# The first transform of batches 1 to 7, from twelve split passes over 128 rows to three sessions of folded 64x64 tiles

## The chip, the cores and the metric

One core of one Trainium2 chip runs the whole kernel in one launch. The metric is the device time of a launch in microseconds (us); lower is better. TensorE (PE) multiplies, VectorE (DVE), ScalarE (ACT) and GpSimd (POOL) work elementwise, and SyncE (SP) issues nearly all transfers, in program order.

## The reference, cut to what matters

```python
X = np.fft.rfft(x, axis=1)                      # x: 8 batches x 3072 x 256, float32
y = np.fft.irfft(X * (filt_r + 1j * filt_i), n=3072, axis=1)
x = y.reshape(8 * 3072, 256)
h = np.maximum(x @ w_in, 0.0)                   # w_in 256 x 2048
x = h * h @ w_out                               # w_out 2048 x 256
# then a soft mixture of 8 experts with 32 slots over all 24576 rows:
#   softmax over the rows gathers slot inputs, softmax over the slots hands the results out
```

The transform of 3072 points is done in two stages, 128 x 24. The first stage is the one that changes: for each of the 24 columns n, a real transform of 128 points over the rows, as a product with a constant 128 x 128 matrix of cosines and sines.

## The kernel before, in words

The main loop (`for P in range(NP + 2)`) runs over 384 pairs. A pair makes two blocks of 128 hidden columns for a chunk of 512 rows: `layer` issues three matmuls per call and four calls per pair, into the two PSUM banks p0 and p1, one bank each per block. `square` (ACT, and POOL for the second block), `turn_h` (a DVE transpose), `logit` (PE, `mm L`) and once per chunk of eight pairs the softmax work (`gather`, `slot_in`, `accum`) follow.

Everything else is put between those matmuls by hand. Time in the schedule is counted in half steps: a pair is two of them, six `layer` matmuls each, and a chunk is 16. A batch is six chunks, 96 half steps. `fft_events` writes, for batch b, when each piece is issued (`put(T, function, ...)`), relative to the start of batch b-1, whose matmuls run meanwhile. Four lists (`dsp`, `late`, `fft`, `w`) are walked by `run_streams` in order of due time. A piece that needs PSUM banks (the table `take`) is issued only when so many of the five side banks are free; otherwise it and all later ones that need banks wait.

Each engine executes its instructions in that written order, SP its transfers too: a store that waits for its data holds up the loads written behind it.

The first stage before, per batch: `load_x` brings x in six transfers of 512 KB (128 partitions, 4 columns n). Twelve times, every 0.9 to 1.5 half steps: `split_x` makes a high part h on ACT and a remainder lo on POOL (both float32r, a reduced format that TensorE runs faster than float32); `mm_a` issues three matmuls of 128x128 by 512 columns into one bank (lines 159 to 161: matrix high times h, matrix low times h, matrix high times lo); `evac_a` copies the bank to SBUF on ACT; `store_a` writes 256 KB to a DRAM scratch S. Later `load_s2` reads S back transposed for the second stage: `mm_b`, `filt` (DVE), `join` (POOL), `mm_g2`, `evac_g2`, `store_g2`, each four times a batch (j = 0 to 3). Batch 0 goes another way, in the head, and has no part in this.

The tiles f8 (1 MB, three buffers) hold x, the filter, S and the output of the second stage in turn; the tiles u (256 KB, eight buffers) held h, lo, the evacuated bank and the products of `filt`.

Of the kernel before, what the change touches and what calls it, by code (L numbers as in the profile page):

```python
# [6 lines left out]
F32 = mybir.dt.float32  # L7
F32R = mybir.dt.float32r
U32 = mybir.dt.uint32
ACTF = mybir.ActivationFunctionType  # L10
ALU = mybir.AluOpType
# [4 lines left out]
D = 256  # L16
N1 = 128
N2 = 24
# [20 lines left out]
def body(tc, x, cA, cAf, fwp, fwd, ivp, inv, flt, cst, w_in, w_out, phi, w1, w2, out):  # L39
    nc = tc.nc  # L40
    sync = nc.sync
    act, vec, gps, pe = nc.scalar, nc.vector, nc.gpsimd, nc.tensor

    def pool(name, bufs=1, space=None, side=None):
        kw = {} if space is None else {"space": space}
        p = tc.tile_pool(name=name, bufs=bufs, side=side, **kw)
        return p, p.__enter__()
# [4 lines left out]
    const_c, const = pool("const")  # L52
# [4 lines left out]
    first_c, first = pool("first")  # L57
# [5 lines left out]
    def F(i):  # L63
        return ST["F0"] + ST["dF"] * i
# [18 lines left out]
    def put0(t, fn, *a):  # L83
        ev0[round(t, 3)].append((fn, a))


    cst_t = const.tile([128, C_END], F32, name="cst_t")
    ca_t = const.tile([128, 2, 128], F32R, name="ca_t")
    ss_t = const.tile([128, 128], F32R, name="ss_t")
    phi_t = const.tile([128, 2, NS], F32, name="phi_t")  # L90
    cI = cst_t[:, C_I:C_I + 128]
# [17 lines left out]
    def side():  # L109
        if G["nsd"]:  # L110
            return G["ps"].tile([128, 512], F32, tag="sd", name="sd", bufs=G["nsd"])
        k = free.pop(0)
        p = G["ps"].tile([128, 512], F32, tag=f"s{k}", name="sd")
        taken[id(p)] = k, p
        return p

    def done(p):

        if id(p) in taken:
            free.append(taken.pop(id(p))[0])  # L120


    def fft_events(b, pl, put, A0, dA, TB, TG, n, st):
        xv = x[b].rearrange("(p n) d -> p n d", n=N2)

        def bank0(k):
            return G["ps"].tile([128, 512], F32, tag=f"q{k}", name="sd", bufs=1)

        def one(tag, shape):
            return pl().tile(shape, F32, tag=tag, name=tag.rstrip("0123456789"), bufs=1)  # L130

        def small(k=None):
            if b == 0:
                return one(k, [128, 2, D])
            return pl().tile([128, 2, D], F32, tag="u", name="u", bufs=n["u"])

        def load_x(sl):
            t = st["x2"] if sl % 2 else wide()
            st["x2"], t = t, t[:, sl % 2]
            st["x", sl] = t  # L140
            sync.dma_start(out=t, in_=xv[:, 4 * sl:4 * sl + 4, :])

        def load_u(u):
            sl, n = divmod(2 * u, 4)
            st["x", sl] = st["big"][:, sl]
            sync.dma_start(out=st["x", sl][:, n:n + 2], in_=xv[:, 2 * u:2 * u + 2, :])

        def split_x(u):
            src = st["x", u // 2][:, 2 * (u % 2):2 * (u % 2) + 2, :]
            h = small().bitcast(F32R)  # L150
            lo = small().bitcast(F32R)
            act.activation(out=h, in_=src, func=ACTF.Copy)  # L152
            gps.tensor_tensor(out=lo, in0=src, in1=h.bitcast(F32), op=ALU.subtract)  # L153
            st["xs", u] = (h, lo)

        def mm_a(u):
            p = side()
            h, lo = st.pop(("xs", u))
            pe.matmul(p, ca_t[:, 0, :], h, start=True, stop=False)  # L159
            pe.matmul(p, ca_t[:, 1, :], h, start=False, stop=False)  # L160
            pe.matmul(p, ca_t[:, 0, :], lo, start=False, stop=True)  # L161
            st["a", u] = p

        def evac_a(u):
            if u == 0:
                st["S"] = dram.tile([N1, N2, D], F32, tag="S", name="S")
            p = st.pop(("a", u))
            o = small()
            act.activation(out=o, in_=p.rearrange("p (a d) -> p a d", d=D), func=ACTF.Copy)
            done(p)  # L170
            st["o", u] = o

        def store_a(u):
            sync.dma_start(out=st["S"][:, 2 * u:2 * u + 2, :], in_=st.pop(("o", u)))


        def wide():
            return pl().tile([128, 2, 4, D], F32, tag="f8", name="f8", bufs=n["f"])
# [201 lines left out]
        if b == 0:  # L380
# [21 lines left out]
            for i in range(8):  # L402
                put((.38, .4, .42, .44)[i] if i < 4 else F(i - 4) + 2.6, load_f, i)
                T = (16.8, 17.2, 20, 22.4, 24.9, 25.3, 27.4, 27.8)[i]
                for s in range(2):
                    put(T + .1 * s, mm_t, i, s)
                    put(T + .3 + .1 * s, evac_t, i, s)
                put(F(i) - 1.2, mm_b, i)
# [4 lines left out]
                put((29.85, 32.3, 34.75, 37.2, 39.9, 41.5, 44.6, 40.5)[i], mm_g, i)  # L413
                T = (31.1, 33.6, 36.1, 38.6, 41.2, 44.7, 45.9, 42.4)[i]
                for c in range(4):
                    put(T, evac_g, i, c)
                put(T + 1.25, store_g, i)
            return

        for sl in range(6):  # L420
            put(A0 + 2 * sl * dA - 5, load_x, sl)
        for u in range(12):
            T = A0 + u * dA
            put(T - 2, split_x, u)
            put(T, mm_a, u)
            put(T + 0.5, evac_a, u)
            put(T + 2.5, store_a, u)
        for j in range(4):
            T = TB[j]
            for k in range(2):  # L430
# [9 lines left out]
            T = TG[j]  # L440
# [423 lines left out]
    streams = {"dsp": [], "late": [], "fft": [], "w": []}  # L864
    heads = dict.fromkeys(streams, 0)

    take = {"warm": 1, "mm_a": 1, "mm_b": 2, "mm_g": 4, "mm_g2": 4, "mm_ai": 1, "gather": 1, "slot_in": 4, "turn_wo": 1, "mm_wf": 1}

    def takes(fn, a):
        if fn is conv_wo and a[1] in (6, 7, 10, 11):  # L870
# [3 lines left out]
    def stream(nm, o=0):  # L874
        def put(t, fn, *a):
            streams[nm].append((t + o, fn, a))
        return put
# [33 lines left out]
        G["fft_c"], G["fft"] = pool("fft", 2)  # L911

    def load_const():
        gps.dma_start(out=ca_t, in_=cA)
        gps.dma_start(out=ss_t, in_=cst[:, C_SS:C_SS + 128])
        sync.dma_start(out=phi_t, in_=phi.rearrange("(k p) s -> p k s", p=128))

# [26 lines left out]
    with tc.manual_schedule():  # L944
        put, late = stream("fft"), stream("late")
        st = {}
        put0(43.3, load_const)
        fft_events(0, lambda: first, put0, 0, 0, 0, 0, None, st)
        out_events(0, st, late)
        def wput(t, *a):  # L950

# [7 lines left out]
        for j in range(4):  # L959
            ts, ops, h, lo = WI[j]  # L960
# [20 lines left out]
        for b in range(1, NB):  # L981
            st = {}
            if b == 1:
                when = (27, .9, [49, 54.5, 65.5, 76.5], [53, 61.5, 70.5, 81.5])
            elif b == 2:
                when = (-14, 1, [5.5, 21.5, 37.5, 53.5], [17.5, 33.5, 49.5, 65.5])
            else:
                when = (-25, 1.5, [1.5, 21.5, 37.5, 53.5], [17.5, 33.5, 49.5, 65.5])
            fft_events(b, lambda: G["fft"], stream("fft", 96 * (b - 1)), *when, dict(f=3, u=8, c=2), st)
            out_events(b, st, late)  # L990
        for c in range(NCH - 1):
# [48 lines left out]
        for P in range(NP + 2):  # L1040
# [15 lines left out]
            if P > NP - 8:  # L1056
                j, odd = divmod(P - NP + 7, 2)
# [17 lines left out]
        st, evac_l, gather, emax, expo, rescale, turn_e, turn_l, slot_in, row_max, row_exp, row_out, store_c = dispatch_events(NCH - 1, None)  # L1075
# [15 lines left out]
        for r in range(4):  # L1091
# [4 lines left out]
            out=fz, in0=run["z"], scalar=st["sc"], in1=st["zb"], op0=ALU.mult, op1=ALU.add  # L1096
# [18 lines left out]
        parts = hs[0] + [dsp.tile([128, 512], F32, tag=t, name="sp") for t in ("lp", "et")]  # L1115
        for r in range(4):
            p = st["S"][r]
# [18 lines left out]
        p = bank("s0")  # L1136
        for j in range(16):
# [3 lines left out]
                start=(j < 4), stop=(j >= 12), tile_position=(0, 32 * c4),  # L1141
# [3 lines left out]
        p = bank("s1")  # L1145
# [31 lines left out]
        def layer2(r, h):  # L1177
# [25 lines left out]
        p = bank("s4")  # L1203
# [6 lines left out]
            out=sr[64:128], in0=p[64:128, 0:D], in1=sr[64:128].bitcast(F32), op=ALU.subtract  # L1210
# [5 lines left out]
        for g in range(NG):  # L1216
            b, o = divmod(g, N2 // 4)
# [3 lines left out]
            for h in range(2):  # L1221
                p = bank(("s0", "s1", "s2", "s3")[ops % 4]).rearrange("p (a d) -> p a d", d=D)
# [19 lines left out]
def _constants():  # L1242
    import numpy as np

    def split(a):
        a32 = a.astype(np.float32)
        h = (a32.view(np.uint32) & np.uint32(0xFFFFF000)).view(np.float32)
        return h, (a - h.astype(np.float64)).astype(np.float32)

    p = np.arange(N1)  # L1250
    j, ri = p // 2, p % 2
    n1 = np.arange(N1)
    ph = 2 * np.pi * ((n1[:, None] * j[None, :]) % N1) / N1
    alt = (-1.0) ** n1
    a = np.where(ri[None, :] == 0, np.cos(ph), -np.sin(ph))
    a[:, 0] = 1.0
    a[:, 1] = alt
    cA = np.stack(split(a), axis=1)
    cAf = a.reshape(N1, 8, 2, 4, 2).transpose(0, 1, 3, 2, 4).reshape(N1, N1)
    ci = np.where(ri[None, :] == 0, np.cos(ph), -np.sin(ph)).T.copy()  # L1260
    ci[0] = 1.0
# [3 lines left out]
    ks = np.zeros((64, 24), np.int64)  # L1265
    ang = np.zeros((64, 24), np.int64)
    for jj in range(64):
        for q in range(24):
            if jj == 0:
                ks[jj, q] = 128 * q if q < 12 else 64 + 128 * (q - 12)  # L1270
                ang[jj, q] = ks[jj, q]
            elif q < 12:
                ks[jj, q] = ang[jj, q] = jj + 128 * q
            else:
                ks[jj, q] = 128 - jj + 128 * (q - 12)
                ang[jj, q] = N - ks[jj, q]
    fw = np.zeros((32, 96, 128))
    iv = np.zeros((32, 128, 96))
# [1 line left out]
    for t in range(32):  # L1280
        for jj in range(2):
            jb = 2 * t + jj
            rr = 48 * jj
            for q in range(24):
# [4 lines left out]
                if jb == 0:  # L1289
                    src = r0 if q < 12 else r1  # L1290
# [25 lines left out]
    for jb in range(64):  # L1316
        t, jj = divmod(jb, 2)
# [77 lines left out]
```

## Time and profile before

| | us |
|---|---|
| median of 3 runs | 1933.9 (1932.58 to 1937.23) |
| the profiled execution, whole | 1935.35 |
| its span, first to last instruction | 1933.6 |
| PE busy in the span | 1900.2 (98%) |
| DVE / ACT / POOL busy | 1196.9 / 1066.5 / 708.9 |
| mean granted TensorE clock | 0.997 of full |

The profile lists busy time by engine, a chain of waits followed back from the last instruction, and groups of instructions by source line. Its matmul ends are modelled, so the distance from one matmul's start to the next one's start says more than a matmul's duration.

### The profile page before, as it was taken

Reading aid. Unit: us, or ns where it says so; the run is one execution under the profiler, and the core shown is the slowest. Engines: PE = TensorE matmul, PEld = TensorE weight load, DVE = VectorE, ACT = ScalarE, POOL = GpSimd, SP = SyncE. Lnnn points to the kernel's source line nnn. Section 1 sums busy time; section 2 is a strip of 40 time slices with the busy share of each in tenths; the row PEclk is TensorE's granted clock in tenths of the full one; section 3 lists DMA queues with packets and bytes.
Section 4 is the critical chain, followed back from the end, with each engine's and each line's share of the span. In section 5 each row is a group of like instructions: output and inputs, shape, how many; then the busy total and the mean of one; then the engine's idle time right before and its main releaser. Section 6 shows DMA issues by size and latency. Waiting matters only on the chain.

```text
span 1933.6 us, 44644 instructions
## 1 busy us (share of the span) xinstructions
PE 1900.2 (98%) x18448; PEld 1321.0 (68%) x18448; DVE 1196.9 (62%) x2209; ACT 1066.5 (55%) x1974; POOL 708.9 (37%) x765
## 2 busy tenths in 40 slices
PE   8999999999999999999999999999999999999987
PEld 6776667666776776766766676676766667676655
DVE  7855656575566646656566655665565655565658
ACT  6764555555654565555555465455745545455535
POOL 4052453343434343334433344333533422222224
PEclk9999999999999999999999999999999999999999
DMA  8634544342334134233424234322442414000589
GB/s 305 208 132 114 164 149 125 81 119 95 117 99 110 48 133 130 77 87 109 131 63 129 69 117 137 88 77 62 151 99 79 110 30 145 13 26 14 163 320 382
DMA packets 139787, 232.27 MB, mean 120 GB/s; under 512 B 13888, under 2 KB 91840, under 8 KB 139584
## 3 DMA queue, kind: packets, MB, share of 16 engines
q1 hardware_dynamic: 138568, 228.08, 38.5%
q8 instruction: 145, 2.38, 0.5%
q10 hardware_dynamic: 728, 1.15, 0.2%
q14 instruction: 58, 0.48, 0.1%
q0 software_dynamic: 288, 0.20, 0.1%
HBM read 151.77 MB, written 77.59 MB: 119 GB/s over the span
## 4 chain that ended last, share of the span: by engine, by line
PE 93%; DVE 3%; DMA 2%; issue 1%; ACT 1%; SPq 0%; ACTq 0%; DVEq 0%
PE p L531 19%; PE p L533 18%; PE p L532 18%; PE sd L683 11%; PE L L558 9%; PE sd L470 4%; PE sd L292 3%; PE sd L211 3%; PE sd L159 1%; PE sd L160 1%; PE sd L161 1%; DVE ct L1029 1%; PE pt L1018 1%; PE pt L1225 1%; DMA x<-x 1%
## 5 line engine op out<-in xcount | busy, mean ns | idle before, releaser
L538 ACT ACTIVATE h<-p 128x512 f32<-128x512 f32 x768 | 459.6, 599 | 547.8 <-PE p L533 524.7
L542 POOL TENSOR_TENSOR h<-h 128x512 f32<-128x512 f32 x375 | 390.7, 1042 | 940.8 <-ACT h L538 855.9
L549 DVE STREAM_TRANSPOSE hT<-h 128x512 f32<-128x512 f32 x768 | 513.9, 692 | 316.7 <-ACT h L540 315.5
L531 PE MATMUL p<-xo,wiH 128*128 128x512 f32 x1534 | 627.6, 409 | 0.6 <-ACT h L538 0.6
L533 PE MATMUL p<-xo,wiL 128*128 128x512 f32 x1534 | 605.9, 395 | 0.0
L532 PE MATMUL p<-xo,wiH 128*128 128x512 f32 x1534 | 605.8, 395 | 0.0
L531 PEld LDWEIGHTS p<-xo,wiH 128*128 128x128 f32 x1534 | 289.1, 188 | 136.4 <-issue 69.6
L533 PEld LDWEIGHTS p<-xo,wiL 128*128 128x128 f32 x1534 | 289.1, 188 | 68.6
L532 PEld LDWEIGHTS p<-xo,wiH 128*128 128x128 f32 x1534 | 289.7, 189 | 57.3
L540 ACT ACTIVATE h<-h 128x512 f32<-128x512 f32 x393 | 248.4, 632 | 12.5
L699 DVE SCALAR_TENSOR_TENSOR ac<-ac,sc,sd 128x512 f32<-128x512 f32 x184 | 129.6, 724 | 201.8 <-PE sd L683 201.8
L683 PE MATMUL sd<-hT,eT 32*32 32x512 f32 x6144 | 215.2, 597 | 3.5 <-issue 2.2
L312 POOL TENSOR_TENSOR u<-u 128x256 f32<-128x256 f32 x224 | 159.2, 741 | 84.9 <-DVE u L303 76.0
L558 PE MATMUL L<-h,wf 128*32 128x512 f32 x1536 | 186.2, 598 | 0.4 <-ACT h L540 0.4
L683 PEld LDWEIGHTS sd<-hT,eT 32*32 32x32 f32 x6144 | 102.1, 103 | 112.2 <-issue 60.7
L303 DVE TENSOR_TENSOR u<-sd,f 128x512 f32<-128x512 f32 x240 | 150.1, 676 | 11.4 <-PE sd L292 10.3
L153 POOL TENSOR_TENSOR u<-f,u 128x512 fp32r<-128x512 f32 x84 | 108.8, 1295 | 103.4 <-ACT u L152 103.1
L607 DVE TENSOR_TENSOR lo<-L,lp 128x512 fp32r<-128x512 f32 x47 | 32.4, 690 | 134.1 <-ACT lp L606 134.1
L221 ACT ACTIVATE f<-sd 128x512 f32<-128x512 f32 x112 | 61.2, 608 | 85.5 <-PE sd L211 85.5
L470 PEld LDWEIGHTS sd<-cst_t,gin 128*128 128x128 f32 x752 | 98.5, 191 | 8.4
L558 PEld LDWEIGHTS L<-h,wf 128*32 128x32 f32 x1536 | 40.1, 109 | 93.2 <-issue 91.5
L470 PE MATMUL sd<-cst_t,gin 128*128 128x128 f32 x752 | 98.9, 274 | 0.0
(148 smaller groups left out, 1508.5 us busy)
## 6 DMA issues: line engine op xcount, KB each, us to landing
f<-flt SPq DMA_DIRECT2D x28, 1024.0 KB
gin<-G SPq DMA_DIRECT2D x47, 512.0 KB
out<-w1t SPq DMA_DIRECT2D x47, 512.0 KB
f<-x SPq DMA_DIRECT2D x42, 512.0 KB
S<-u SPq DMA_DIRECT2D x84, 256.0 KB
f<-S SPq DMA_DIRECT2D x112, 192.0 KB
G<-f SPq DMA_DIRECT2D x112, 192.0 KB
iv<-inv SPq DMA_DIRECT2D x56, 128.0 KB
```

The costliest lines, as they stand in the source:

```text
L303: vec.tensor_tensor(out=u, in0=p.rearrange("p (h d) -> p h d", d=D), in1=f[:, 2 * r + k:2 * r + k + 1, :].to_broadcast([128, 2, D]), op=AL ...
L312: gps.tensor_tensor(out=a[:, h, :], in0=a[:, h, :], in1=b[:, 1 - h, :], op=ALU.add if h else ALU.subtract)
L470: pe.matmul(p[:, 128 * a:128 * a + 128], t[:, a, 128 * k:128 * k + 128], cI, start=True, stop=True,)
L531: pe.matmul(p, wh, x[:, 0, kk, :], start=(kk == 0), stop=False)
L532: pe.matmul(p, wh, x[:, 1, kk, :], start=False, stop=False)
L533: pe.matmul(p, wl, x[:, 0, kk, :], start=False, stop=(kk == 1))
L538: act.activation(out=h, in_=p, func=ACTF.Relu, scale=2.0 ** -8)
L540: act.activation(out=h, in_=h, func=ACTF.Square)
L542: gps.tensor_tensor(out=h, in0=h, in1=h, op=ALU.mult)
L549: vec.transpose(hT[c][:, 2 * i + k, :], h2[P, k])
L558: pe.matmul(lg[c][32 * n:32 * n + 32, :], wf[:, f, :], h2.pop((P + n // 2, n % 2)), start=(f < 4), stop=(f >= FT - 4), tile_position=(0, 3 ...
L683: pe.matmul(S[r][32 * a:32 * a + 32, :], e[rows, o:o + 32], h[rows, :, o:o + 32], start=(t == 0), stop=(t == 3), tile_position=(32 * r, 32 ...
```

## The change

x is loaded with the two halves of the 128 rows side by side: partition 64g + p holds, for rows p and p + 64, two columns n. DVE adds the halves into a tile u, POOL subtracts them in place. The even outputs of the 128-point transform need the sums alone, the odd ones the differences alone, so `mm_a` multiplies them by two 64 x 64 float32 matrices: eight matmuls of 64x64 by 512 columns per session, four tile positions (two row halves g, two output halves e), into four banks. A session does 8 of the 24 columns n; there are three per batch. ACT copies the four banks back over the x tile, and two stores of 512 KB write it to S. The constants are reordered to fit (even outputs first), and `ca_t` is loaded by SP instead of POOL.

Each session has its own three times (load, fold, matmul). The second stage of batch 1 begins at half step 47 instead of 49, that of batch 2 at 13.5 instead of 5.5, with its first inverse at 18.5 instead of 17.5.

```diff
-    ca_t = const.tile([128, 2, 128], F32R, name="ca_t")
+    ca_t = const.tile([128, 2, 64], F32, name="ca_t")
...
-        def load_x(sl):
-            t = st["x2"] if sl % 2 else wide()
...
-            sync.dma_start(out=t, in_=xv[:, 4 * sl:4 * sl + 4, :])
+        def load_x(s):
+            st["x", s] = t = wide()
+            for k in range(2):
+                for g in range(2):
+                    n = 8 * s + 4 * k + 2 * g
+                    sync.dma_start(
+                        out=t[64 * g:64 * g + 64, k].rearrange("p (h n) d -> p h n d", h=2), in_=xh[:, :, n:n + 2, :]
+                    )
...
-            act.activation(out=h, in_=src, func=ACTF.Copy)
-            gps.tensor_tensor(out=lo, in0=src, in1=h.bitcast(F32), op=ALU.subtract)
...
-            pe.matmul(p, ca_t[:, 0, :], h, start=True, stop=False)
-            pe.matmul(p, ca_t[:, 1, :], h, start=False, stop=False)
-            pe.matmul(p, ca_t[:, 0, :], lo, start=False, stop=True)
...
+        def fold_x(s, k):
+            t = st["x", s][:, k]
+            st["xe", s, k] = e = small()
+            vec.tensor_tensor(out=e, in0=t[:, 0:2], in1=t[:, 2:4], op=ALU.add)
+            gps.tensor_tensor(out=t[:, 2:4], in0=t[:, 0:2], in1=t[:, 2:4], op=ALU.subtract)
+
+        def mm_a(s):
+            st["a", s] = p = [[side() for g in range(2)] for k in range(2)]
+            for k in range(2):
+                parts = st.pop(("xe", s, k)), st["x", s][:, k, 2:4]
+                for e in range(2):
+                    for g in range(2):
+                        rows = slice(64 * g, 64 * g + 64)
+                        pe.matmul(
+                            p[k][g][64 * e:64 * e + 64, :], ca_t[rows, e, :], parts[e][rows],
+                            start=True, stop=True, skip_group_check=True, tile_position=(64 * g, 64 * e),
+                        )
...
-        for u in range(12):
-            T = A0 + u * dA
-            put(T - 2, split_x, u)
-            put(T, mm_a, u)
-            put(T + 0.5, evac_a, u)
-            put(T + 2.5, store_a, u)
+        for s, (TL, TF, T) in enumerate(TA):
+            put(TL, load_x, s)
+            for k in range(2):
+                put(TF + k, fold_x, s, k)
+                for g in range(2):
+                    put(T + 0.5 + 0.5 * k, evac_a, s, k, g)
+                put(T + 2 + 0.5 * k, store_a, s, k)
+            put(T, mm_a, s)
...
-    take = {"warm": 1, "mm_a": 1, "mm_b": 2, "mm_g": 4, "mm_g2": 4, "mm_ai": 1, "gather": 1, "slot_in": 4, "turn_wo": 1, "mm_wf": 1}
+    take = {"warm": 1, "mm_a": 4, "mm_b": 2, "mm_g": 4, "mm_g2": 4, "mm_ai": 1, "gather": 1, "slot_in": 4, "turn_wo": 1, "mm_wf": 1}
...
-        gps.dma_start(out=ca_t, in_=cA)
+        sync.dma_start(out=ca_t, in_=cA)
...
-                when = (27, .9, [49, 54.5, 65.5, 76.5], [53, 61.5, 70.5, 81.5])
+                when = ([(22, 25, 28), (24, 29, 33.5), (27.5, 32, 36.5)], [47, 54.5, 65.5, 76.5], [53, 61.5, 70.5, 81.5])
             elif b == 2:
-                when = (-14, 1, [5.5, 21.5, 37.5, 53.5], [17.5, 33.5, 49.5, 65.5])
+                when = ([(-19, -15.5, -10.5), (-11, -7, -3), (-5.5, -3, 0)], [13.5, 21.5, 37.5, 53.5], [18.5, 33.5, 49.5, 65.5])
             else:
-                when = (-25, 1.5, [1.5, 21.5, 37.5, 53.5], [17.5, 33.5, 49.5, 65.5])
+                when = ([(-35, -31, -26.5), (-23, -19, -14.5), (-19.5, -15.5, -10.5)], [1.5, 21.5, 37.5, 53.5], [17.5, 33.5, 49.5, 65.5])
```

## Rows read from the trace of the kernel before

**Rows 1.** The page: busy us and share by engine; the group of slot_in's matmuls.

```profile
PE 1900.2 (98%) x18448; PEld 1321.0 (68%) x18448; DVE 1196.9 (62%) x2209; ACT 1066.5 (55%) x1974; POOL 708.9 (37%) x765
...
L683 PE MATMUL sd<-hT,eT 32*32 32x512 f32 x6144 | 215.2, 597 | 3.5 <-issue 2.2
```

**Rows 2.** Busy time by engine in 300 to 540 us: length, then each engine.

```profile
300.00:540.00 240.00, 240.00 (x2331) 166.70 (x2330) 147.70 (x277) 132.92 (x243) 95.68 (x102) 1.00 0.40 113
```

**Rows 3.** Groups by line, the old first stage: count, busy us, mean ns, idle before.

```profile
L153 POOL TENSOR_TENSOR u<-f,u 128x512 fp32r<-128x512 f32 x84 | 108.8, 1295 | 103.4 <-ACT u L152 103.1
...
L152 ACT ACTIVATE u<-f 128x512 fp32r<-128x512 f32 x84 | 52.3, 623 | 0.0
...
L159 PE MATMUL sd<-u,ca_t 128*128 128x512 f32 x84 | 34.3, 408 | 0.0
```

**Rows 4.** Timeline of PE around one unit of the old first stage: start, length.

```profile
1380.31 0.39 PE L159 MATMUL sd<-u,ca_t 128*128 128x512 f32 x1
...
1381.01 0.39 PE L531 MATMUL p<-xo,wiH 128*128 128x512 f32 x1
```

**Rows 5.** Timeline of PE around two logit calls, float32 in four column tiles.

```profile
1382.86 0.40 PE L533 MATMUL p<-xo,wiL 128*128 128x512 f32 x1
1383.19 1.92 PE L558 MATMUL L<-h,wf 128*32 128x512 f32 x16
1385.04 0.50 PE L159 MATMUL sd<-u,ca_t 128*128 128x512 f32 x1
1385.38 0.39 PE L160 MATMUL sd<-u,ca_t 128*128 128x512 f32 x1
```

**Rows 6.** Timeline of PE around one inverse (L211), float32 in eight tiles.

```profile
214.23 0.40 PE L533 MATMUL p<-xo,wiL 128*128 128x512 f32 x1
214.56 1.98 PE L211 MATMUL sd<-u,iv 32*64 32x256 f32 x64
...
216.81 0.39 PE L532 MATMUL p<-xo,wiH 128*128 128x512 f32 x1
```

**Rows 7.** Groups by line: elementwise operations on two SBUF operands, on POOL and DVE.

```profile
L542 POOL TENSOR_TENSOR h<-h 128x512 f32<-128x512 f32 x375 | 390.7, 1042 | 940.8 <-ACT h L538 855.9 <-issue 50.9 <-DVE hT L549 34.0
...
L806 DVE TENSOR_TENSOR wa<-wa,we 128x512 f32<-128x512 f32 x4 | 2.8, 692 | 0.1
```

**Rows 8.** SP's own instructions of one line: count, shortest, median, longest ns.

```profile
L141 SPq DMA_DIRECT2D f<-x x42: 327/424/952, 100.8 to 1376.6; - x42
```

**Rows 9.** Timeline of PE in batch 1's first inverse, then its busy time by stretch.

```profile
185.42 0.86 PE L211 MATMUL sd<-u,iv 32*64 32x256 f32 x6
...
187.74 3.05 PE L211 MATMUL sd<-u,iv 32*64 32x256 f32 x58 [1.46 <-DVE u L303]
...
188.40:191.80 3.40, 3.40 (x49) 2.26 (x31) 0.40 (x1) 1.01 (x2) 0.69 (x2) 0.51 0.12 17
```

**Rows 10.** Timeline of PE in one slot_in, then busy time by stretch around it.

```profile
153.54 4.41 PE L683 MATMUL sd<-hT,eT 32*32 32x512 f32 x123
...
160.18 1.05 PE L683 MATMUL sd<-hT,eT 32*32 32x512 f32 x5 [2.24 <-issue]
...
152.00:156.00 4.00, 4.00 (x98) 1.64 (x105) 0.99 (x2) 0.39 (x1) 1.04 (x1) 1.00 1.07 283
...
161.10:164.60 3.50, 3.50 (x10) 2.76 (x9) 0.00 (x0) 0.47 (x1) 0.00 (x0) 0.51 0.02 5
```

**Rows 11.** The instruction queue: packets, MB, share; the page, then 144 to 160 us.

```profile
q8 instruction: 145, 2.38, 0.5%
...
q8 instruction: 1, 0.02, 0.6%
```

**Rows 12.** Timeline of PE: batch 1's last inverse, five half steps after its forward part.

```profile
263.65 2.53 PE L211 MATMUL sd<-u,iv 32*64 32x256 f32 x64
```

**Rows 13.** The chain of waits: slot_in of two neighbouring chunks.

```profile
361.48 4.39 PE sd L683 x120
...
398.58 4.39 PE sd L683 x120
```

More of the change, by code (lines that the diff above doesn't have):

```diff
@@ L120, in done, with fft_events @@
             free.append(taken.pop(id(p))[0])
-    def fft_events(b, pl, put, A0, dA, TB, TG, n, st):
+    def fft_events(b, pl, put, TA, TB, TG, n, st):
         xv = x[b].rearrange("(p n) d -> p n d", n=N2)
+        xh = x[b].rearrange("(h p n) d -> p h n d", h=2, n=N2)
         def bank0(k):
@@ L135, in small @@
             return pl().tile([128, 2, D], F32, tag="u", name="u", bufs=n["u"])
-        def load_x(sl):
-            t = st["x2"] if sl % 2 else wide()
-            st["x2"], t = t, t[:, sl % 2]
-            st["x", sl] = t
-            sync.dma_start(out=t, in_=xv[:, 4 * sl:4 * sl + 4, :])
+        def load_x(s):
[6 more added lines that the diff above has]
+                    )
         def load_u(u):
@@ L146, in load_u @@
             sync.dma_start(out=st["x", sl][:, n:n + 2], in_=xv[:, 2 * u:2 * u + 2, :])
[L148 to L151, printed above, removed]
-            act.activation(out=h, in_=src, func=ACTF.Copy)
-            gps.tensor_tensor(out=lo, in0=src, in1=h.bitcast(F32), op=ALU.subtract)
[L154 to L158, printed above, removed]
-            pe.matmul(p, ca_t[:, 0, :], h, start=True, stop=False)
-            pe.matmul(p, ca_t[:, 1, :], h, start=False, stop=False)
-            pe.matmul(p, ca_t[:, 0, :], lo, start=False, stop=True)
-            st["a", u] = p
@@ L164, in evac_a @@
-        def evac_a(u):
-            if u == 0:
-                st["S"] = dram.tile([N1, N2, D], F32, tag="S", name="S")
[L167 to L174, printed above, removed]
+        def fold_x(s, k):
[3 more added lines that the diff above has]
+            gps.tensor_tensor(out=t[:, 2:4], in0=t[:, 0:2], in1=t[:, 2:4], op=ALU.subtract)
@@ L177, in wide, with evac_a, store_a @@
+        def evac_a(s, k, g):
+            p = st["a", s][k][g]
+            act.activation(
+                out=st["x", s][:, k, 2 * g:2 * g + 2], in_=p.rearrange("p (n d) -> p n d", d=D), func=ACTF.Copy
+            )
+            done(p)
+        def store_a(s, k):
+            if s + k == 0:
+                st["S"] = dram.tile([N1, N2, D], F32, tag="S", name="S")
+            n = 8 * s + 4 * k
+            sync.dma_start(out=st["S"][:, n:n + 4, :], in_=st["x", s][:, k])
         def wide():
@@ L418, in fft_events @@
             return
-        for sl in range(6):
-            put(A0 + 2 * sl * dA - 5, load_x, sl)
-        for u in range(12):
-            T = A0 + u * dA
-            put(T - 2, split_x, u)
-            put(T, mm_a, u)
-            put(T + 0.5, evac_a, u)
-            put(T + 2.5, store_a, u)
+        for s, (TL, TF, T) in enumerate(TA):
[6 more added lines that the diff above has]
+            put(T, mm_a, s)
         for j in range(4):
@@ L947, in body @@
         put0(43.3, load_const)
-        fft_events(0, lambda: first, put0, 0, 0, 0, 0, None, st)
+        fft_events(0, lambda: first, put0, 0, 0, 0, None, st)
         out_events(0, st, late)
@@ L1243, in _constants @@
     import numpy as np
[L1245 to L1248, printed above, removed]
     p = np.arange(N1)
-    j, ri = p // 2, p % 2
+    js = np.concatenate([np.arange(0, 64, 2), np.arange(1, 64, 2)])
+    j, ri = js[p // 2], p % 2
     n1 = np.arange(N1)
@@ L1257, in _constants @@
     a[:, 1] = alt
-    cA = np.stack(split(a), axis=1)
+    cA = np.tile(a[:64].reshape(64, 2, 64), (2, 1, 1))
     cAf = a.reshape(N1, 8, 2, 4, 2).transpose(0, 1, 3, 2, 4).reshape(N1, N1)
@@ L1272, in _constants @@
             elif q < 12:
-                ks[jj, q] = ang[jj, q] = jj + 128 * q
+                ks[jj, q] = ang[jj, q] = js[jj] + 128 * q
             else:
-                ks[jj, q] = 128 - jj + 128 * (q - 12)
+                ks[jj, q] = 128 - js[jj] + 128 * (q - 12)
                 ang[jj, q] = N - ks[jj, q]
```

## Prediction

> **What bounds the kernel now.** I read the page first: PE is busy 98% of the span [rows 1]. A modelled matmul end can hide a gap, so the timeline of PE comes next, read by starts: a `layer` matmul of 512 columns follows the one before after 0.23 us [rows 4], and from 300 to 540 us PE has no hole at all, while DVE works 148 of 240 us, ACT 133 and POOL 96 [rows 2]. In the steady part the time is the sum of what PE is given. The waits show where it is not: two holes, both in the stretch of batch 1, that I come back to. A chunk of 16 half steps lasts 398.58 - 361.48 = 37.1 us [rows 13], so a half step is about 2.3 us.
>
> **The change part by part.**
>
> *Removed from PE.* A unit of the old first stage is three matmuls, from 1380.31 to 1381.01 = 0.70 us [rows 4]. There are 84 units [rows 3]: 7 batches of 12. 84 x 0.70 = 58.8 us.
>
> *Added on PE.* A session is eight float32 matmuls of 512 columns in four tile positions. The trace has no 64x64 tile. It has two neighbours. Two logit calls are eight float32 matmuls of 512 columns in four column tiles, each issued as two instructions (x16): between the last `layer` matmul at 1382.86 and the second matmul after, at 1385.38, lie 2.52 us, of which 2 x 0.23 would have passed without them: 2.06 us [rows 5]. That holds both changes of tile shape. An inverse is 64 instructions of 256 columns in eight tiles, the same columns per tile, and it divides the rows too: 216.81 - 214.23 - 0.46 = 2.12 us [rows 6]. So four row-and-column tiles should run beside each other as eight do. I take 2.06: 21 x 2.06 = 43.3 us. Lower end: the 16 instructions alone, 1385.04 - 1383.19 = 1.85 us [rows 5], 38.9 us. Upper end: the two row halves take turns, 2 x 1.85 + 0.21 = 3.9 us, 82 us. Net on PE: -15.5 us, between -20 and +23.
>
> *Taken from ACT and POOL, given to DVE.* ACT loses 84 splits of 623 ns, 52 us [rows 3]; its 84 evacuations stay. POOL loses 84 subtractions of 1295 ns [rows 3] and gets 42, between 1042 [rows 7] and 1295 ns. DVE gets 42 sums of 692 ns [rows 7], 29 us, four per chunk at most. The slack in rows 2 hides it: I count nothing. Without that cover a fold would be late for its session; from its first sum to its matmuls it has 3 to 5 half steps, 7 to 12 us, for two sums (1.4 us) and two differences (2.6 us). Behind a sum that waits for its load stand the transposes and accumulations of DVE, and on them hang h tiles (five buffers) and side banks.
>
> *Transfers.* Per batch SP issued 6 loads and 12 stores; now 12 and 6, of the same bytes. The count of 18 stays, at about 0.4 us each [rows 8]. `ca_t` on SP's queue in the head costs one more issue, 0.4 us, ahead of stores that wait for their evacuation: nothing. What changes is bunching. In batches 3 to 7 SP reaches session 0's stores (512 KB), the next load of `gin` (512 KB), and sessions 1 and 2's loads (2 MB) one behind the other, the last as soon as those stores have landed and freed its buffer; at 283 GB/s [rows 10] that is 11 us of full queues, and `slot_in`, due at 9.5 in each chunk, falls into it.
>
> *A wait that goes.* In batch 1 the first inverse, due four half steps after its forward part, started at 185.42, waited 1.46 us for `filt` on DVE, and then the granted clock was 0.51 for 3.4 us, the 1.2 GHz level, which costs half of that: 1.7 us [rows 9]. With the forward part at 47 the distance is six half steps. -3.2 us (bounds -4 and 0). The next thing late there is the forward part at 54.5, which needs the same banks: not moved by this.
>
> *Waits that come.* (a) Batch 2's first inverse stands five half steps behind its forward part. Batch 1's last inverse has that distance and took 2.53 us against the usual 1.98 [rows 6, 12]: +0.5 us. (b) Its session at half step -3 takes four banks that DVE empties just then: +0.5 us, between 0 and 2. (c) Instruction supply. At 157.9 PE stood still 2.24 us inside `slot_in`, waiting for nothing that the profile shows, and the clock fell to 0.51 afterwards [rows 10]. The instruction queue moved 145 packets, 2.38 MB [rows 11]; PE's 36,896 instructions [rows 1] over 145 are 254 each. From 144 to 160 us only one arrived [rows 11], while the data queues were at 1.07 of full [rows 10]. I read the hole as PE out of instructions: `slot_in` uses 256 in 4.4 us. Price: 2.24 + 1.7 = 3.9 us. It needs a block to fall due within some 30 instructions of a `slot_in` under full queues. The bunching above makes that a real chance in six batches; it depends on the phase of 256 that nobody can read here. I leave the one that is there, and add half of one: +2 us (bounds -3.9, the old one gone, and +23, six new ones).
>
> The Trainium skill (DMA: Bandwidth & Descriptors, on queues, rings and completion order) says that each transfer engine takes turns between its queues packet by packet. By that rule a block of instructions would wait for one packet only, (c) would be 0 and the forecast 1916. The rows speak against it: one block in 16 us under full queues and a hole in the engine that needed it.
>
> Sum: -15.5 - 3.2 + 0.5 + 0.5 + 2 = -15.7 us. The profiled execution took 1935.35 us, 1.8 more than its span: less 15.7, 1919.7. It stood 1.4 above the median of 1933.9; for the median that is 1918.
>
> **The rivals.**
>
> *Bigger gain* (chance 0.07): no new wait at all and the old hole in `slot_in` gone: -15.5 - 3.2 - 3.9 = -22.6, 1911. For it: of the 48 calls of `slot_in` (6144 matmuls at 128 a call [rows 1, 10]) this is the only one with such a hole: the group stood 3.5 us in all. Against it: the same stores and second-stage loads precede that one still.
>
> *PE runs out of instructions* (0.11): the bunched loads starve `slot_in` in several later batches. At 3.9 us each, -15.5 - 3.2 + 1 = -17.7 is eaten by four and a half; three give 1928, six 1940. For it: the hole at 157.9. Against it: one hole in 48.
>
> *The four tiles do not overlap* (0.07), the case on the slower side: if row halves take turns, a session is 3.9 us and the sum -58.8 + 82 - 3.2 + 3 = +23: 1957. It decides from 2.8 us a session (58.8 / 21). For it: no row of 64x64; the weights of four tiles must be loaded ahead. Against it: rows 6, eight tiles with four row groups at full rate.
>
> *Late folds* (0.07): `mm_a` now hangs on a chain load, DVE, POOL (the difference overwrites what the sum reads, so POOL follows DVE), and PE waits in order. 0.9 us per session cancels the gain: 1934. Likeliest in batch 2, where the third session's load stands 2.5 half steps before its fold. Against it: in steady state the loads are issued ahead of their time.
>
> *Forecast* (0.68): 1918, itself good for 1912 to 1924.
>
> **How the numbers follow.** A change under 0.3%, 5.8 us, cannot be told from none: faster means below 1928.1, slower above 1939.7. Faster: 0.68 + 0.07, and 0.03 and 0.02 from starved supply and late folds: 0.80. Same: 0.05 and 0.03 of these two: 0.08. Slower: tiles 0.07, 0.03 and 0.02: 0.12. The range of 8 in 10 takes in the bigger gain and the first starved cases: 1909 to 1935.
>
> **What would show it.** In the profile after: x336 float32 instructions of 64x64, in groups of 16 between two `layer` matmuls with 2.0 to 2.2 us between the starts (3.9 would be the tile rival); no wait on DVE in front of batch 1's first inverse and no clock drop behind it; holes of 2 us inside `slot_in` put down to "issue", with a clock of 0.5 after them, counted by batch (the supply rival); PE waiting in front of `mm_a` for POOL or DVE (late folds). ACT 50 us and POOL about 55 us less busy, DVE 29 us more, without effect on the span. The prediction is wrong if the span falls by less than 10 us with sessions of 2.1 us, or if another engine ends the waits.

## The result and the profile after

The changed kernel takes 1913.38 us (median of 4 runs, 1911.62 to 1914.04) against 1934.16 for the kernel before, measured again beside it: a ratio of 0.9891 with an interval of 0.9879 to 0.9903, 20.8 us less. The forecast was 1918, inside its own range. The profiled execution took 1911.62 us, its span 1909.6: 23.7 and 24.0 less than the profiled execution of before, which stood above its median while this one is the lowest of four.

The page: busy time by engine, and the group of `slot_in`, now at line 690 [rows 1].

```profile
PE 1879.9 (98%) x18532; PEld 1281.2 (67%) x18532; DVE 1219.8 (64%) x2251; ACT 1024.6 (54%) x1890; POOL 657.5 (34%) x722
...
L690 PE MATMUL sd<-hT,eT 32*32 32x512 f32 x6144 | 214.6, 597 | 1.3 <-DVE eT L669 1.3
```

PE is 20.3 us less busy and 3.7 us less idle; the 2.2 us of "issue" in `slot_in` are gone. PE still has no hole in the steady part, with 240 of 240 us [rows 2]:

```profile
300.00:540.00 240.00, 240.00 (x2460) 161.49 (x2459) 152.11 (x283) 125.54 (x229) 89.49 (x98) 1.00 0.43 113
```

So most of the gain is the sum of what PE is given. The timeline of PE around one session shows it [rows 4, 5]:

```profile
450.31 0.40 PE L540 MATMUL p<-xo,wiL 128*128 128x512 f32 x1
...
450.64 0.65 PE L165 MATMUL sd<-u,ca_t 64*64 64x512 f32 x2
450.65 0.65 PE L165 MATMUL sd<-f,ca_t 64*64 64x512 f32 x2
451.12 0.59 PE L165 MATMUL sd<-u,ca_t 64*64 64x512 f32 x2
451.13 0.60 PE L165 MATMUL sd<-f,ca_t 64*64 64x512 f32 x2
...
452.52 0.50 PE L538 MATMUL p<-xo,wiH 128*128 128x512 f32 x1
452.86 0.39 PE L539 MATMUL p<-xo,wiH 128*128 128x512 f32 x1
```

The four tiles run together: pairs of rows (each x2, two row halves) start 10 ns apart, the next pass 0.43 to 0.48 us later. From the last `layer` matmul to the second one after lie 2.55 us, less 2 x 0.23: 2.09 us, and 2.08 in most of the 13 sessions that stand so. Six of the 21 sessions stand right behind a logit call, and there the change into tiles is already paid:

```profile
477.35 0.39 PE L540 MATMUL p<-xo,wiL 128*128 128x512 f32 x1
477.67 1.92 PE L565 MATMUL L<-h,wf 128*32 128x512 f32 x16
479.52 0.65 PE L165 MATMUL sd<-u,ca_t 64*64 64x512 f32 x2
...
481.74 0.39 PE L539 MATMUL p<-xo,wiH 128*128 128x512 f32 x1
```

481.74 - 477.35 = 4.39, less 0.46 and the logit call's 2.06 [rows 5]: 1.87 us. The other two stand behind short matmuls of another piece (line 477) and take 1.96.

The two places where PE stood still before, the one `slot_in` and batch 1's first inverse [rows 9, 10], each with a `layer` matmul behind it; then the stretches of 152 to 156 and 178 to 182 us (length, busy time of PE, PEld, DVE, ACT, POOL, granted clock, DMA share, GB/s):

```profile
151.80 4.46 PE L690 MATMUL sd<-hT,eT 32*32 32x512 f32 x128
...
158.40 0.39 PE L538 MATMUL p<-xo,wiH 128*128 128x512 f32 x1
...
178.81 1.98 PE L218 MATMUL sd<-u,iv 32*64 32x256 f32 x64
...
181.52 0.39 PE L538 MATMUL p<-xo,wiH 128*128 128x512 f32 x1
```

```profile
152.00:156.00 4.00, 4.00 (x128) 1.92 (x104) 0.00 (x0) 0.00 (x0) 0.00 (x0) 1.00 0.98 248
...
178.00:182.00 4.00, 4.00 (x74) 2.80 (x73) 1.84 (x4) 2.36 (x5) 0.55 (x1) 1.00 0.19 34
```

`slot_in` runs through in 4.46 us although the data queues are nearly as full as before (0.98 of their time), the inverse waits for nothing, and the clock is 1.00 in both stretches. What each place gave back is read by starts, up to a `layer` matmul behind the slow stretch. The same two matmuls in the kernel before:

```profile
164.90 0.40 PE L531 MATMUL p<-xo,wiH 128*128 128x512 f32 x1
...
192.04 0.39 PE L531 MATMUL p<-xo,wiH 128*128 128x512 f32 x1
```

From the start of `slot_in` to the tenth `layer` matmul behind it passed 164.90 - 153.54 = 11.36 us, now 158.40 - 151.80 = 6.60: 4.8 less. From the start of the inverse to the fourth `layer` matmul behind it passed 192.04 - 185.42 = 6.62 us, now 181.52 - 178.81 = 2.71: 3.9 less.

One wait is new. In batch 1's last inverse [rows 12] eight matmuls come 0.50 us late, behind a join on POOL:

```profile
253.05 2.25 PE L218 MATMUL sd<-u,iv 32*64 32x256 f32 x56
255.80 0.66 PE L218 MATMUL sd<-u,iv 32*64 32x256 f32 x8 [0.50 <-POOL u L319]
```

It spans 255.80 + 0.66 - 253.05 = 3.41 us instead of 2.53: 0.9 more.

| where the time went | us |
|---|---|
| 84 old units, 0.70 each | -58.8 |
| 21 sessions: 13 x 2.08, 2 x 1.96, 6 x 1.87 | +42.2 |
| first inverse of batch 1 and the clock after it | -3.9 |
| hole in `slot_in` and the clock after it | -4.8 |
| batch 1's last inverse | +0.9 |
| the head, to the first `layer` matmul (54.19, now 54.54 us) | +0.4 |
| sum (the span fell by 24.0) | -24.0 |

The table is of the two profiled executions. The medians lie 20.8 us apart, and which of the terms are smaller in the other executions no trace shows.

### The profile page after: what moved, and what is told of

It reads as the page before. It is cut to its first block, busy times and chain, and to the rows that moved or that the text cites. A ratio compares the mean times of both kernels' runs of the same rounds, so it can differ in the third digit from the quotient of the medians.

```text
span 1909.6 us, 44626 instructions
## 1 busy us (share of the span) xinstructions
PE 1879.9 (98%) x18532; PEld 1281.2 (67%) x18532; DVE 1219.8 (64%) x2251; ACT 1024.6 (54%) x1890; POOL 657.5 (34%) x722
## 4 chain that ended last, share of the span: by engine, by line
PE 94%; DMA 2%; DVE 2%; issue 1%; ACT 1%; POOL 0%; SPq 0%; POOLq 0%; DVEq 0%; ACTq 0%
PE p L538 20%; PE p L539 18%; PE p L540 18%; PE sd L690 11%; PE L L565 9%; PE sd L477 4%; PE sd L299 3%; PE sd L218 3%; PE sd L165 2%; DVE ct L1036 1%; PE pt L1025 1%; PE pt L1232 1%; DMA x<-x 1%; PE sd L339 1%; PE sd L625 1%
## 5 line engine op out<-in xcount | busy, mean ns | idle before, releaser
L486 ACT ACTIVATE xo<-sd 128x512 fp32r<-128x512 f32 x96 | 57.4, 598 | 62.5 <-PE sd L477 62.5
```

## Experiments

**Does the later second stage of batch 1 remove the first inverse's wait, and what is it worth?** My theory: the distance from forward part to inverse does it. One run does that alone on the kernel before, one undoes it in the kernel after.

```diff
-                when = (27, .9, [49, 54.5, 65.5, 76.5], [53, 61.5, 70.5, 81.5])
+                when = (27, .9, [47, 54.5, 65.5, 76.5], [53, 61.5, 70.5, 81.5])
```

> The kernel before with one number changed: the second stage of batch 1 begins at half step 47 instead of 49. Theory (the first inverse waited because it stood four half steps behind its forward part): the 1.46 us wait and the 3.4 us at the 1.2 GHz level go, -3.2 us, some 1931. Rival (DVE is behind at that place whatever the distance): within 0.5 us of the kernel before, and the wait is still in front of the inverse.

1930.33 us against 1934.15, ratio 0.9986 (0.9975 to 0.9997). The wait is gone and the clock stayed up: from the inverse's start to the fourth `layer` matmul behind it pass 2.71 us instead of 6.62, 3.9 less.

```profile
184.75 1.98 PE L211 MATMUL sd<-u,iv 32*64 32x256 f32 x64
...
187.46 0.39 PE L531 MATMUL p<-xo,wiH 128*128 128x512 f32 x1
```

The hole in `slot_in` is still there but smaller, 1.1 us, and no slow clock follows it (columns: us in total, times, longest):

```profile
PE sd L683 <- issue: 1.1, 1, 1.1
```

The other way round, in the kernel after (47 back to 49):

> The changed kernel with the second stage of batch 1 back at half step 49. Theory: the wait and the clock drop return, +3.2 us, some 1916.6. Rival (with a lighter ACT and POOL the inverse no longer waits at four half steps): within 0.5 us of the changed kernel, 1913.4.

1915.65 us, 2.3 above the kernel after; ratio to before 0.9906 (0.9889 to 0.9924). The wait and 3.4 us at the 1.2 GHz level are back:

```profile
178.93 0.83 PE L218 MATMUL sd<-u,iv 32*64 32x256 f32 x6
181.32 3.29 PE L218 MATMUL sd<-u,iv 32*64 32x256 f32 x58 [1.56 <-DVE u L310]
...
185.64 0.39 PE L538 MATMUL p<-xo,wiH 128*128 128x512 f32 x1
```

```profile
181.80:185.20 3.40, 3.40 (x52) 2.34 (x37) 0.59 (x1) 0.60 (x2) 0.87 (x2) 0.50 0.14 20
```

185.64 - 178.93 = 6.71, 4.0 more than the 2.71 of the kernel after. The edit's two half steps are the cause. By starts they are worth 3.9 and 4.0 us, more than the term of 3.2; the medians say 3.8 (with the smaller hole in it) and 2.3.

**Is the hole in `slot_in` instruction supply, and does the bunching starve it?** PE's instructions come in blocks of some 254; where a block's edge falls depends on how many instructions precede it. So I moved the phase, with nearly the same warm-up work in the head cut into more matmuls: by 128 instructions in the kernel before, to move the edge away from `slot_in`, and by 200 in the kernel after, to move it there.

```diff
-            for _ in range(6):
-                pe.matmul(p[:, 0:416], cI, cst_t[:, 0:416], start=True, stop=True)
+            for _ in range(38):
+                pe.matmul(p[0:32, 0:66], cI[:, 0:32], cst_t[:, 0:66], start=True, stop=True)
```

> The kernel before, with the six warm-up matmuls of 416 columns in the head replaced by 38 of 66 columns: the same columns, 128 more PE instructions ahead of the main loop, nothing else. Theory (the hole in slot_in at 157.9 us is PE out of instructions, and 254 of them come per block): the block falls due half a block earlier, ahead of the full queues, and the hole with its clock drop is gone, -3.9 us, some 1930. Rival (the hole belongs to the work at that place): it stays at the same slot_in, 1934.

1932.82 us, ratio 0.9990 (0.9979 to 1.0001): the hole of that `slot_in` is gone, and from its start to the tenth `layer` matmul behind it pass 6.59 us (155.72 to 162.31) instead of 11.36. But over the whole kernel the time gained is not told from none: the main loop starts some 1.6 us later (as it does in the profiled execution with 47, whose head is unchanged), and a `slot_in` at 320 us now has a hole of 0.44 us. The first inverse of batch 1 waits as before, yet the clock stays at 1.00 behind it:

```profile
185.14 2.06 PE L211 MATMUL sd<-u,iv 32*64 32x256 f32 x58 [1.74 <-DVE u L303]
```

```profile
185.20:188.60 3.40, 3.40 (x64) 2.69 (x65) 1.01 (x2) 1.38 (x3) 1.29 (x2) 1.00 0.02 5
```

The same in the kernel after, 56 matmuls of 44 columns (+200 instructions):

> The changed kernel, with the six warm-up matmuls of 416 columns in the head replaced by 56 of 44 columns: 200 more PE instructions ahead of the main loop. Theory (instruction supply): a block now falls due at the start of a slot_in under full transfer queues, in batch 1 or in a batch with bunched loads, and a hole of 1.5 to 2.5 us with a clock drop appears, +3 to +4 us, some 1917, twice that if two fall so. Rival (the folded kernel has no such hole for another reason): no hole, 1913.4.

1914.13 us, ratio 0.9900 (0.9882 to 0.9919). No hole, against my expectation. By the count of PE's instructions the next block was due as `slot_in` started, at 153.4 us; it was served at 155.8, 2.4 us late, and that was in time. In the kernel before the block was served at 157.2. Its due time there follows from the run with swapped loads below, which has the same instructions in the same order and was served this block 1.2 us ahead of `slot_in`: due by 152.3, so at least 4.9 us late. In the run with 47 it was at least 4.2 us late by the same reckoning, and the hole 1.1 us. So an edge at the head of `slot_in` is not enough: 2.4 us late cost nothing there, 4.2 did. In the unshifted kernel after the block had come at 148.8 us, ahead of `slot_in`.

Two runs then put 1 MB more of loads in front of S's loads in that place, with the edge shifted into `slot_in` and without.

```diff
+        def load_more():
+            for i in range(4):
+                sync.dma_start(out=small(), in_=flt[i, :, 0:2])
...
+            if b == 1 and j == 0:
+                put(T - 5.25, load_more)
```

> The kernel of after_phase (200 more PE instructions, so that a block of instructions falls due as chunk 1's slot_in begins) with 1 MB more of loads, read by nobody, between the filter and the S loads of batch 1's second stage: the transfer queues stay full some 3.6 us longer, to about 160 us, beyond the 157.8 at which PE runs out. Theory (a hole needs both, a block due at the start of a slot_in and queues that stay full until it ends): a hole of 1 to 3 us in that slot_in and a clock drop behind it, +3 to +5 us against after_phase, some 1918. Rival (the block comes 2.4 us late at most, however much is queued): no hole, 1914.

1913.47 us, ratio 0.9889 (0.9875 to 0.9904). No hole, though the queues were full until 160 us; the block due at 154.0 was served at 155.9, 1.9 us late:

```profile
154.03 4.46 PE L696 MATMUL sd<-hT,eT 32*32 32x512 f32 x128
```

```profile
152.00:156.00 4.00, 4.00 (x84) 1.39 (x84) 1.31 (x2) 0.74 (x2) 1.04 (x1) 1.00 0.94 343
...
156.00:160.00 4.00, 4.00 (x86) 2.45 (x70) 0.75 (x1) 0.00 (x0) 0.00 (x0) 1.00 1.08 283
```

The theory that a block waits until the queues have drained falls: 4 us of full queues followed, and the block came all the same.

> The changed kernel with the same 1 MB of loads that nobody reads, at the same place. Theory (its block falls due some 40 instructions ahead of slot_in, when these loads are not yet queued): no hole, 1913.4 within 0.5. Rival (more queued data starves PE or delays the second stage by itself): a hole there too, or a wait in front of the second stage, +2 us or more.

1913.41 us, ratio 0.9891 (0.9875 to 0.9908), no hole, as expected: the control.

The late block of the kernel before was served behind S's small pieces (1 KB each). The last run of this kind lets the filter load go behind them, so that other transfers stand there:

```diff
-            put(T - 5.5, load_f2, j)
+            put(T - (4.9 if b + j == 1 else 5.5), load_f2, j)
```

> The kernel before, with batch 1's first loads of the second stage in the other order: the four loads of S (pieces of 1 KB) ahead of the filter's 1 MB (pieces of 4 KB), so that the queues are as full at chunk 1's slot_in but drain the filter. Instruction count and phase as in the kernel before. Theory (it is the S loads' small pieces that keep the block of instructions waiting 3.7 us; behind larger ones it comes 2 us late, in time): no hole in that slot_in, the wait for filt stays, some 1930.5. Rival (any full queue does): the hole stays at 2 us, 1934.

1932.81 us, ratio 0.9992 (0.9983 to 1.0001). No hole:

```profile
154.34 4.46 PE L683 MATMUL sd<-hT,eT 32*32 32x512 f32 x128
```

From the start of this `slot_in` to the tenth `layer` matmul pass 6.59 us, as in the run with the phase moved, and again the whole gain is not told from none. The block was served at 153.1, in time, though the queues were full then (1.06 of their time from 153 to 154 us) and moved S's 1 KB pieces. So neither full queues nor small pieces alone make a block late, and my theory of the pieces falls too. That the hole goes when the block comes in time is borne out; what makes a block come in time in one trace and 1.9 or 4.9 us late in others stays open. The first inverse waited 1.53 us here and, as in the run with the phase moved, the clock did not fall.

**Do the tiles overlap whatever the order, and what does a session cost by itself?** First the eight matmuls reordered so that the two banks of one tile follow each other; then each session issued twice.

```diff
-            for k in range(2):
-                parts = st.pop(("xe", s, k)), st["x", s][:, k, 2:4]
-                for e in range(2):
-                    for g in range(2):
+            both = [(st.pop(("xe", s, k)), st["x", s][:, k, 2:4]) for k in range(2)]
+            for e in range(2):
+                for g in range(2):
+                    for k in range(2):
+                        parts = both[k]
```

> The changed kernel with the eight matmuls of a session in another order: the two columns halves k of one tile position follow each other, then the next position. Same work. Theory (the four tiles run beside each other only because neighbouring matmuls stand on different tiles, PE issuing in order): the second matmul of a pair waits for the first, a session grows from 1.9 us to between 3.4 and 4.3, +33 to +50 us, 1946 to 1964. Rival (each tile takes its next matmul whatever stands between): 1913.

1915.01 us, ratio 0.9904 (0.9884 to 0.9924). Twenty of the 21 sessions are 0.02 us longer, one 0.4, and the start pattern is the same:

```profile
451.93 0.66 PE L166 MATMUL sd<-u,ca_t 64*64 64x512 f32 x2
451.96 0.65 PE L166 MATMUL sd<-f,ca_t 64*64 64x512 f32 x2
452.42 0.60 PE L166 MATMUL sd<-u,ca_t 64*64 64x512 f32 x2
452.44 0.60 PE L166 MATMUL sd<-f,ca_t 64*64 64x512 f32 x2
```

The tiles of the second row start 30 ns after those of the first although a second matmul of the first tile stands between them in the program. Had each waited for the one written before it, that would have cost a pass; the rival, that each tile takes its own next matmul, held. Whether the chip does this or the order was already changed when the program was built, no run shows.

```diff
-            for k in range(2):
-                parts = st.pop(("xe", s, k)), st["x", s][:, k, 2:4]
+            both = [(st.pop(("xe", s, k)), st["x", s][:, k, 2:4]) for k in range(2)]
+            for k in (0, 1, 0, 1):
+                parts = both[k]
```

> The changed kernel with each session's eight matmuls issued twice (the second set writes the same banks again). Theory (a session is 1.72 us of streaming in four tiles side by side and 0.2 to 0.35 us for the two changes of tile shape): +21 x 1.72 = +36 us, 1949.5. Rival (the tiles overlap only in part and the rest of the gain came from elsewhere): +60 us or more, above 1973.

1951.6 us, 38.2 above the kernel after. The sessions' own rows explain 36.1 of it:

```profile
460.71 0.40 PE L541 MATMUL p<-xo,wiL 128*128 128x512 f32 x1
...
464.97 0.39 PE L540 MATMUL p<-xo,wiH 128*128 128x512 f32 x1
```

464.97 - 460.71 - 0.46 = 3.80 us for a doubled session, 1.72 more than 2.08: four passes of 0.43 us for eight matmuls without a change of tile shape. A session of 2.08 is that plus 0.36; behind a logit call (1.87) only 0.15 is added. Were the row halves to take turns, the second set would take 3.4.

**Do the folds cost anything?** One run leaves the sums and differences out (the matmuls read the loaded halves as they are), one moves the fold of batch 2's first session two half steps later, clear of batch 1's last joins.

```diff
-            st["xe", s, k] = e = small()
-            vec.tensor_tensor(out=e, in0=t[:, 0:2], in1=t[:, 2:4], op=ALU.add)
-            gps.tensor_tensor(out=t[:, 2:4], in0=t[:, 0:2], in1=t[:, 2:4], op=ALU.subtract)
+            st["xe", s, k] = t[:, 0:2]
```

> The changed kernel without the sums on DVE and the differences on POOL: the matmuls read the two halves as loaded, so the transform is not computed. Theory (both are hidden beside PE, except where DVE's two-operand sum runs beside POOL's joins ahead of batch 2's first inverse, 1.4 us): 1912 to 1913.4. Rival (sessions wait for their folds, or DVE's sums push other work late): 1908 or less.

1912.54 us, ratio 0.9891 (0.9877 to 0.9906): by the medians 42 sums and 42 differences together cost under 1 us. What the traces show of it is in one place. The timelines of POOL and of DVE in the kernel after, at batch 1's last joins (line 319):

```profile
253.44 2.30 POOL L319 TENSOR_TENSOR u<-u 128x256 f32<-128x256 f32 x2 [1.42 <-DVE u L310]
```

```profile
253.29 0.68 DVE L155 TENSOR_TENSOR u<-f 128x512 f32<-128x512 f32 x1
...
254.51 0.64 DVE L155 TENSOR_TENSOR u<-f 128x512 f32<-128x512 f32 x1
```

Without folds, and then with the fold later:

```profile
254.85 1.42 POOL L317 TENSOR_TENSOR u<-u 128x256 f32<-128x256 f32 x2 [1.43 <-DVE u L308]
```

```diff
-                when = ([(-19, -15.5, -10.5), (-11, -7, -3), (-5.5, -3, 0)], [13.5, 21.5, 37.5, 53.5], [18.5, 33.5, 49.5, 65.5])
+                when = ([(-19, -13.5, -10.5), (-11, -7, -3), (-5.5, -3, 0)], [13.5, 21.5, 37.5, 53.5], [18.5, 33.5, 49.5, 65.5])
```

> The changed kernel with the fold of batch 2's first session two half steps later (-13.5), past batch 1's last inverse. Theory (DVE's sum of two SBUF operands holds up POOL's joins, which that inverse waits for): the two joins take 1.4 us again instead of 2.3, the inverse 2.5 instead of 3.3, -0.8 us, some 1912.5; the session does not wait. Rival (the joins are late because of the half steps alone): the inverse stays at 3.3 us.

1911.73 us, ratio 0.9881 (0.9861 to 0.9900).

```profile
253.22 2.53 PE L218 MATMUL sd<-u,iv 32*64 32x256 f32 x64
```

```profile
253.61 1.42 POOL L319 TENSOR_TENSOR u<-u 128x256 f32<-128x256 f32 x2 [1.43 <-DVE u L310]
```

The two joins take 1.42 us without a sum beside them and 2.30 with, and the inverse is back at 2.53. Both runs take the differences away too, but in the kernel after these run on POOL only behind the joins, from 255.71 us on; and in the last run DVE works beside the joins as well, on transposes, at no cost to them. So the sums cause the 0.9 us. The Trainium skill (SBUF — State Buffer, "Who interferes with whom") says that a DVE instruction with two SBUF inputs contends with a GpSimd instruction that reads SBUF. The trace agrees: the joins are longer by 0.88 us. Over the whole kernel the sums (line 155) range from 644 to 1383 ns.

**A version past both.** The profile after has two waits left in the stretches that the change touches: the one above, and 0.43 us in `mm_b` at 184.54. This run gives both more distance.

```diff
-                when = ([(22, 25, 28), (24, 29, 33.5), (27.5, 32, 36.5)], [47, 54.5, 65.5, 76.5], [53, 61.5, 70.5, 81.5])
+                when = ([(22, 25, 28), (24, 29, 33.5), (27.5, 32, 36.5)], [47, 55.5, 65.5, 76.5], [53, 62.5, 71.5, 82.5])
...
-                when = ([(-19, -15.5, -10.5), (-11, -7, -3), (-5.5, -3, 0)], [13.5, 21.5, 37.5, 53.5], [18.5, 33.5, 49.5, 65.5])
+                when = ([(-19, -15.5, -10.5), (-11, -7, -3), (-5.5, -3, 0)], [13.5, 21.5, 37.5, 53.5], [19.5, 33.5, 49.5, 65.5])
```

> The changed kernel with five due times moved by one half step: batch 1's second forward part to 55.5 and its last three inverses to 62.5, 71.5 and 82.5, batch 2's first inverse to 19.5. Theory (the two waits left in batch 1 are for banks that ACT has not emptied at 183 us, 0.9 us, and for joins that POOL has not finished at 253 us, 1.4 us): both go, -2.3 us, some 1911. Rival (the waits move along with the due times): 1913.4.

1910.82 us (1910.05 to 1911.65), ratio 0.9883 (0.9866 to 0.9899), against 1913.38 for the kernel after; the groups by line show both waits gone (0.0 idle; the kernel after had 0.5 and 0.4):

```profile
L218 PE MATMUL sd<-u,iv 32*64 32x256 f32 x1792 | 55.5, 380 | 0.0
L299 PE MATMUL sd<-f,fw 48*32 48x256 f32 x1792 | 55.0, 379 | 0.0
```

The medians come from different comparisons and the intervals overlap; what is shown is that the two waits are gone. By PE's starts the stretch that holds both, 178.48 to 299.02 us in the kernel after and 179.15 to 297.84 here, is 1.85 us shorter.

## Why the prediction held, and where it did not

*PE's account* (forecast -15.5): -16.6, right in kind, 1.1 us short. 2.06 us for a session was read from logit calls, and 13 sessions take 2.08. The term that was mis-sized is the 21 x 2.06: a session behind a logit call does not pay the change of tile shape again, 6 x 0.2 us.

*First inverse* (-3.2): the mechanism was right, shown by doing and undoing it; by starts it was 3.9, because wait and slow stretch were priced by modelled ends. That the clock falls behind such a wait was read from one trace as a rule; the two runs of the kernel before with a wait of 1.74 and 1.53 us and a clock of 1.00 say that it does not always.

*Waits that come, (a) and (b)* (+0.5 each): wrong place. Batch 2's first inverse takes 1.98 us, and the session at half step -3 waits for nothing. The 0.9 us that did come is in batch 1's last inverse, because "I count nothing" for DVE left out that a sum slows the POOL operation beside it. The sum of these terms was about right by luck.

*Instruction supply, (c)* (+2): the wrong step. That the hole is PE waiting for a block is borne out: it is gone in every trace in which the block came in time. Its price was 4.8 us by starts, not 3.9. But "I leave the one that is there" failed: in the profiled execution after, the hole is gone, -4.8 where the term said +2. The added half hole did not come either. Why it went is not shown. In the kernel before it goes with another number of instructions ahead, and also with the same number and two loads exchanged; in the kernel after an edge put back at the head of `slot_in` did not bring it back. So the shift of the blocks and the changed transfers are both still possible causes. Nor is it shown what the hole costs in a usual execution: the two runs of the kernel before that lost it have medians 1.3 and 2.8 us below that of the kernel before, neither told from none.

The Trainium skill (DMA: Bandwidth & Descriptors, "Queues, rings and completion order") has each transfer engine take turns between its queues packet by packet; by that rule (c) was 0, nearer to the result than my +2. The runs do not bear the rule out as I used it: under full queues blocks were served 1.9 to at least 4.9 us late, one in time, and with 1 MB more queued no later. No run says why.

*Rivals.* The bigger gain (1911) is what the profiled execution shows, with the old hole gone and the 0.9 us on top; the median, 1913.4, lies between it and the forecast, nearer to the former. In the profiled pair the sum fell 8.3 us short (15.7 against 24.0), 6.8 of it in (c); that the medians lie only 20.8 apart, and the forecast within 5 us of the median, is luck. The tile rival is refuted by the session's own rows and by 1.72 us per doubled session. Late folds: no wait in front of any `mm_a`; their 0.9 us a session to cancel the gain was reckoned without (a) to (c), with them it is 15.7 / 21 = 0.75. ACT and POOL are 41.9 and 51.4 us less busy and DVE 22.9 more, near the forecast's 50, 55 and 29; the span shows of it the 0.9 us alone.

## What to carry to other kernels

Where PE is busy without a hole, price a change by start-to-start distances of the nearest tiled group, and look at what stands in front of each insertion: a second tiled group behind a first one is cheaper. Price a wait and the slow clock behind it by starts as well, up to a matmul at full speed. A hole that the profile puts down to "issue" under full queues can belong to a block of instructions that comes late, not to the code there: here a change of the instruction count removed one and left a smaller one elsewhere, and a change of the order of two loads removed it too. So it is a term of either sign. Work moved to an engine with slack still has a price if it slows its neighbour in the one stretch where that one is late.

## What the runs showed of the hardware

In the one other order tried inside a group of tiles, two matmuls of the same tile in a row cost no pass (451.93 and 451.96 us). A wait of 1.46 and 1.56 us in the first inverse was followed by 3.4 us at the lower clock level, one of 1.74 and one of 1.53 in the same place by none; neither the length of the wait nor its place decides it alone. A block of PE's instructions due at the head of `slot_in` could come 2.4 us late at no cost; at least 4.2 us late it cost a stop of 1.1 us, at least 4.9 us late one of 2.24. Two joins on POOL took 2.30 us beside a sum of two SBUF operands on DVE, 1.42 without.
